# Background steps held in order on three more engines, and the q features of the down product cut into small steps

## The chip, the cores and the metric

The kernel runs on one core of one Trainium2 chip. The metric is the time of the program on the device in microseconds (us), smaller is better. The kernel before took 2384.36 us, the median of three runs (2380.04 to 2385.91).

## The reference

```
xn  = layernorm(x)                                  # x: 2048 rows of 1024
qkv = xn @ wqkv                                     # 1024 -> 3 * 1024, 32 heads of 32
pq, pk   = q @ w_phi, k @ w_phi                     # per head
phi_q = concat(softmax(pq), softmax(-pq))           # phi_k alike; 64 features a head
kv  = phi_k^T v;   z = sum over rows of phi_k
o   = (phi_q kv) / (phi_q z + 1e-6)
s   = o @ wo
h   = sigmoid(xn @ w_gate) * (xn @ w_up)            # 1024 -> 3584
g   = silu(h @ w_down)                              # 3584 -> 1024
out = x + s * g
```

All tensors are fp32.

## The kernel before, in words

**Arithmetic.** An fp32 product is three matmuls of numbers cut to a high and a low part (`mm3`, lines 142 to 144). So every operand is first split: ScalarE copies the high part (line 133), VectorE subtracts it from the source to get the low part (line 134). Each large product (x by wqkv, x by gate and up, h by down) is a seven-product Strassen-Winograd scheme over 2x2 blocks; the products are called B11, T2, T3, B21, T1, T4 and B22, and their results are added in PSUM (eight banks of 128x512) or in SBUF, some of them by way of DRAM.

**Stages, in order of time.** (1) A first list, FIRST, whose instructions stand in an order written out by hand on all engines. (2) The projection to q, k, v for one half of the rows (`PROJ`, column block c = 0). Its results are evacuated by `project`'s inner function, lines 608 to 636; ScalarE copies a bank to a buffer y (lines 612 and 620) and the y is stored to the DRAM tensor `qkv_d`. The buffers y come from a ring, `yps[0]`, of two half slots, both in slot 47. (3) Pass 0 of the gate and up products. (4) The projection for c = 1. (5) Pass 1 of gate and up, whose evacuations are `keep_bank` (ScalarE, line 1328, store to `m_d`), `seed` (ScalarE, line 1324, which fills a bank with a partial result), and `h_direct` (sigmoid on ScalarE, line 1361, product on VectorE, line 1363). (6) Pass 2 (`nest`), which finishes gate and up. (7) The down product: 112 steps `dsteps`, of 24 matmuls each up to the last product, B22, where a step has 12; `down_prep` loads and splits operands for the steps to come (tiles `x` and `w` read from slot `fa`), `evacuate` empties the banks after each product. (8) Attention, the output projection, and the output.

**Background work.** Beside the matmuls of stages 2 to 6 runs work on other data. It is cut into steps and put into a plan: `later(n, f)` runs f at the n-th `tick` from now, and `tick()` is called once for every 12 matmuls. `k_steps` (line 719) plans the chain for 128 rows of k and v: `k_load` (SyncE's DMA queue, lines 678 to 680), `k_extremes` (VectorE max and min, lines 643, 644), `k_spread` (653, 654), the exponential (ScalarE, 657), `k_inverses` (662, 663), `k_scale` (699), `k_low` (707, 709) and `kv_products` (8 matmuls, line 715). The sums of weight blocks for the Strassen scheme (GpSimd) and their loads are planned in the same way (`glu_group`, `fetch_operand`, `wd_sums`, `x_nest_load` and so on).

**Order of instructions.** Each engine, and SyncE's DMA queue, takes its instructions strictly in order. Where no list is written by hand, a scheduler sets that order from the program's order and from when it thinks an instruction can start. `tc.issue_after(x)` holds the instructions of the block, on the engine of x, behind x. Before, `tick` holds the background steps behind the last matmul, which speaks of TensorE only; during pass 0 the loads are held behind the last traced load too (`loads_after`). On VectorE, ScalarE and the queue the scheduler is free to put a background instruction ahead of instructions of the main work that were traced earlier.

**The q features in the down product.** `q_task(t, hb)` (line 930) does 128 rows by 512 columns of phi_q over its denominator: load, for half of the tasks the whole chain of features (`features`, lines 638 to 664), a product with z on GpSimd (941), a reduction and small operations on VectorE (944 to 950), a scaling on GpSimd (953) and a store. There are 32 tasks, and the step loop of the down product traces one whole task every 2.4 steps, held behind the last operand split. Both GpSimd operations cover 128x1024.

**Evacuation in the down product** (lines 1678 to 1699). B11: ScalarE copies the bank to u1. B21: a sigmoid by ScalarE from the bank and a product by VectorE with the bank (`gate_out` with `fused`, lines 1674 and 1675), for all eight banks after the last step. T2 and T3: VectorE adds bank and u1. T4: VectorE adds bank and u1 to a buffer, later a sigmoid and a product by GpSimd. The banks start afresh in B11, T2, T3 and T1 and go on adding in the others.

Of the kernel before, what the change touches and what calls it, by code (L numbers as in the profile page):

```python
# [18 lines left out]
P = 128  # L19
# [30 lines left out]
def hedgehog_glu_kernel(  # L50
# [62 lines left out]
    EARLY = 12  # L113

# [50 lines left out]
    loads_fixed = []  # L165

    def loads_after():

        return tc.issue_after(last_load[0]) if loads_fixed else nullcontext()
# [119 lines left out]
    fblock = {K: ((6, 7), (36, 37), (52, 53), (36, 37)), Q: ((50, 51), (52, 53)) * 2}  # L289
# [168 lines left out]
    def glu_group():  # L458
# [25 lines left out]
        if not groups:  # L484
            kept = [b for b in raw_free if not any(b is o for o in spare)]
            raw_free.clear()
            raw_free.extend(kept)

# [414 lines left out]
    eqr = Ring((50, 51))  # L903
    qraw = Ring([slots[53][:, 1]])
    zb = whole(54)
# [24 lines left out]
    def q_task(t, hb):  # L930
        e, ez = whole(eqr.next()), whole(52)
        if t < CTT:
            nc.sync.dma_start(e, e_d[t, hb])
            r = small.tile([P, 32], F32, name=f"r{t}{hb}", tag="r", bufs=2)
            nc.sync.dma_start(r, r_d[t, hb])
        else:
            p = qraw.next()
            nc.sync.dma_start(p, qkv_d[Q, t, hb])
            r = features(f"q{t}{hb}", p, e)
        st = small.tile([P, 5, 16], F32, name=f"sa{t}{hb}", tag="sa", bufs=2)  # L940
        nc.gpsimd.tensor_mul(ez, e, zb)  # L941
        d2 = st[:, 0:2].rearrange("p t h -> p (t h)")
        r2 = st[:, 2:4].rearrange("p t h -> p (t h)")
        nc.vector.tensor_reduce(d2, ez.rearrange("p (g d) -> p g d", d=DH), axis=AX.X, op=ALU.add)  # L944
        nc.vector.tensor_mul(d2, d2, r)  # L945
        den = st[:, 4]
        nc.vector.tensor_reduce(den, d2.rearrange("p (h t) -> p h t", t=2), axis=AX.X, op=ALU.add)
        nc.vector.tensor_scalar_add(den, den, EPS_DEN)
        nc.vector.reciprocal(den, den)
        nc.vector.tensor_mul(r2.rearrange("p (h t) -> p h t", t=2), r.rearrange("p (h t) -> p h t", t=2),  # L950
                             den[:, :, None].to_broadcast([P, 16, 2]))
        e3 = e.rearrange("p (g d) -> p g d", d=DH)
        nc.gpsimd.tensor_mul(e3, e3, r2[:, :, None].to_broadcast([P, 32, DH]))  # L953
        nc.sync.dma_start(e_d[t, hb], e)
# [438 lines left out]
    def begin_pass(p):  # L1393
# [12 lines left out]
        elif p == 1:  # L1406
            gates_r.items = halves(45, 46)
            gates_r.n = 0
            at = 1
# [15 lines left out]
    def x_nest_load(th):  # L1425
        for h in range(2):
            nc.sync.dma_start(slots[((52, 53), (43, 44))[th][h]], xr_d[T1, :, 4 * th + 2 * h:4 * th + 2 * h + 2])

    def x_nest_parts(h):

        lo, hi = slice(0, 256), slice(256, HB)
        first, second = slots[52 + h], slots[43 + h]
# [7 lines left out]
    def x_nest_split(i):  # L1440
# [8 lines left out]
        if i == T1:  # L1449
            uvfree.extend(halves(52))  # L1450
            raw_free.extend(spare)
            spare.clear()
# [81 lines left out]
    for n, (kind, c, what, i) in enumerate(ops):  # L1534
# [3 lines left out]
        if kind == "proj":  # L1538
            if n == 8 or (c and (what, i) == (PROJ[0], B11)):
                loads_fixed.clear()  # L1540
# [48 lines left out]
        if m == 0:  # L1589
# [5 lines left out]
            loads_fixed[:] = [True] if phase == 0 else []  # L1595
# [43 lines left out]
        elif phase == 1 and f == NJ - 1:  # L1639
# [5 lines left out]
            else:  # L1645
                for b in (3, 5):
                    block(f"x{b}", 4 * b, 4, F32)
                uvfree.extend(halves(12, 13, 14, 15, 20, 21, 22, 23, 51, 45, 46, 47))
                hs_r.items = halves(48, 49, 50)
# [14 lines left out]
    block("fb", 44, 3, F32R)  # L1664
# [13 lines left out]
    def evacuate(i, p):  # L1678
# [5 lines left out]
        elif i == B21:  # L1684
            gate_out(yr.next(), t, 0, b)
        elif i == T2:
            nc.vector.tensor_add(u1[p], u1[p], b)
        elif i == T3:
            nc.vector.tensor_add(u2[p], u1[p], b)
        elif i == T4:  # L1690
            y = yr.next()
            nc.vector.tensor_add(y, u1[p], b)  # L1692
            gate_out(y, t + 4, 0)
        elif i == T1:
            nc.vector.tensor_add(u2[p], u2[p], b)
            gate_out(u2[p], t + 4, 1)
# [4 lines left out]
    wd_late, wd_kept = {}, []  # L1701
    for k, j in enumerate(range(10, NJ)):
        for part in range(3):
            wd_late.setdefault(6 * k + 1 + 2 * part, []).append((j, part))

    def wd_steps(n):
        for j, part in wd_late[n]:
            if part == 0:
                wd_kept[:] = wd_parts(j, halves(43, 38))
            else:  # L1710
# [227 lines left out]
```

## Time and profile before

| what | value |
|---|---|
| median of 3 runs (lowest to highest) | 2384.36 us (2380.04 to 2385.91) |
| the profiled execution | 2383.35 us |
| its span, first to last instruction | 2381.6 us |
| TensorE (PE) busy | 2353.0 us, 99% |
| VectorE (DVE) busy | 1654.7 us, 69% |
| ScalarE (ACT) busy | 1155.2 us, 49% |
| GpSimd (POOL) busy | 1025.5 us, 43% |
| mean granted TensorE clock | 0.996 |

How to read the profile's lines: a group's row has line, engine, operation, output <- inputs, count, then busy us and mean ns of one, then idle us of the engine just before them and what ended it. In a timeline row the start and the duration in us come first; brackets at the end hold the idle time before the instruction and the instruction that released it. A row of stretches of time ("windows") has the stretch and its length, then the busy us and the instruction count of PE, PEld (weight loads), DVE, ACT and POOL, the granted TensorE clock as a share of full speed, the busy share of the DMA engines and GB/s. A matmul of 128x512 is issued about every 0.23 us; its shown duration of 0.39 us overlaps the next.

### The profile page before, as it was taken

The numbers are of one execution on the slowest core, as the hardware profiler recorded it, in microseconds if no ns is written. First come the engines' busy times: TensorE is split into PE (matmuls) and PEld (weight loads), VectorE is DVE, ScalarE is ACT, GpSimd is POOL, SyncE is SP. The second block draws the span as 40 slices with busy tenths as digits, with TensorE's granted clock in tenths as the row PEclk, the third lists the DMA queues.
The fourth block names the chain that finished last, engine by engine and source line by source line (L and its number), as shares of the span: only waits on it lengthen the run. The fifth ranks groups of instructions, "written<-read, shape, count | busy, mean of one in ns | idle before, by whom it ended". The sixth has DMA issues, their size and how long they took to land. (4 is left out here: it accounts for less than half of the span.)

```text
span 2381.6 us, 32170 instructions
## 1 busy us (share of the span) xinstructions
PE 2353.0 (99%) x10900; PEld 1958.7 (82%) x10900; DVE 1654.7 (69%) x2099; ACT 1155.2 (49%) x1814; POOL 1025.5 (43%) x673
## 2 busy tenths in 40 slices
PE   9999999999999999999999999999999999999999
PEld 8887888888888888777888878888878888888887
DVE  8615676665588844677765575666898988877776
ACT  7344554454544645545555445453433334455553
POOL 0224236711132044555431588876533334424566
PEclk9999999999999999999999999999999999999999
DMA  8788999975687787777764889889766666876665
GB/s 294 250 311 335 358 349 351 394 262 191 191 289 247 270 289 245 257 276 253 241 232 155 303 285 307 299 301 354 254 232 229 227 221 217 284 255 243 203 206 180
DMA packets 288309, 633.55 MB, mean 266 GB/s; under 512 B 36752, under 2 KB 37008, under 8 KB 283536
## 3 DMA queue, kind: packets, MB, share of 16 engines
q1 hardware_dynamic: 288144, 631.50, 76.4%
q8 instruction: 85, 1.39, 0.2%
q14 instruction: 80, 0.66, 0.1%
HBM read 378.40 MB, written 252.97 MB: 265 GB/s over the span
## 5 line engine op out<-in xcount | busy, mean ns | idle before, releaser
L142 PE MATMUL bank<-x,w 128*128 128x512 f32 x2304 | 900.8, 391 | 13.6 <-ACT fc L1328 4.5
L143 PE MATMUL bank<-x,w 128*128 128x512 f32 x2304 | 899.6, 390 | 0.2 <-DVE x L134 0.2
L144 PE MATMUL bank<-x,w 128*128 128x512 f32 x2304 | 898.2, 390 | 0.0
L134 DVE TENSOR_TENSOR w<-fa,w 128x512 fp32r<-128x512 f32 (+1 forms) x440 | 427.5, 978 | 261.0 <-ACT w L133 248.3
L142 PEld LDWEIGHTS bank<-x,w 128*128 128x128 f32 x2304 | 434.1, 188 | 107.0 <-ACT fc L1328 6.0
L144 PEld LDWEIGHTS bank<-x,w 128*128 128x128 f32 x2304 | 433.9, 188 | 90.5 <-DVE w L134 0.4
L143 PEld LDWEIGHTS bank<-x,w 128*128 128x128 f32 x2304 | 434.2, 188 | 89.1 <-DVE x L134 0.6
L133 ACT CAST w<-fa 128x512 fp32r<-128x512 f32 (+1 forms) x440 | 297.7, 680 | 364.2 <-PE bank L143 275.8
L142 PE MATMUL bank<-w,x 128*128 128x512 f32 x708 | 278.7, 394 | 7.1 <-ACT fc L620 4.7
L143 PE MATMUL bank<-w,x 128*128 128x512 f32 x708 | 276.9, 391 | 0.9 <-DVE w L1195 0.9
L144 PE MATMUL bank<-w,x 128*128 128x512 f32 x708 | 276.4, 391 | 0.0
L142 PEld LDWEIGHTS bank<-w,x 128*128 128x128 f32 x708 | 133.4, 188 | 35.5 <-ACT fc L620 5.9
L144 PEld LDWEIGHTS bank<-w,x 128*128 128x128 f32 x708 | 133.4, 188 | 28.4 <-DVE x L1185 0.3
L143 PEld LDWEIGHTS bank<-w,x 128*128 128x128 f32 x708 | 133.5, 189 | 27.3 <-DVE w L1195 1.3
L1328 ACT COPY fc<-bank 128x512 f32<-128x512 f32 x168 | 97.1, 583 | 119.2 <-PE bank L144 50.5
L941 POOL TENSOR_TENSOR fc<-fc 128x1024 f32<-128x1024 f32 x32 | 80.7, 2521 | 160.5 <-ACT fc L657 103.2
L134 DVE TENSOR_TENSOR x<-fa,x 128x512 fp32r<-128x512 f32 x112 | 115.4, 1031 | 23.9 <-ACT x L133 23.8
L133 ACT CAST x<-fa 128x512 fp32r<-128x512 f32 x112 | 69.3, 619 | 89.4 <-DMA fa<-w_down 44.7
L953 POOL TENSOR_TENSOR fc<-fc,sa 128x1024 f32<-128x1024 f32 x32 | 70.4, 2200 | 81.3 <-DVE sa L950 76.7
L134 DVE TENSOR_TENSOR p<-fc,p 128x512 fp32r<-128x512 f32 (+1 forms) x67 | 56.7, 854 | 48.9 <-ACT p L133 48.6
L657 ACT ACTIVATE fc<-fc 128x1024 f32<-128x1024 f32 x48 | 50.9, 1060 | 60.7 <-DVE fc L654 47.7
L134 DVE TENSOR_TENSOR x<-fb,x 128x1024 fp32r<-128x1024 f32 (+1 forms) x40 | 51.7, 1309 | 33.1 <-ACT x L133 32.7
(368 smaller groups left out, 3401.0 us busy)
## 6 DMA issues: line engine op xcount, KB each, us to landing
m_d<-fc SPq DMA_DIRECT2D x168, 256.0 KB, 4.4
fa<-h_d SPq DMA_DIRECT2D x84, 512.0 KB, 4.3
fa<-wf_d SPq DMA_DIRECT2D x32, 1024.0 KB, 6.4
x<-m_d SPq DMA_DIRECT2D x122, 256.0 KB, 4.7
h_d<-fc SPq DMA_DIRECT2D x98, 256.0 KB, 4.7
fc<-e_d SPq DMA_DIRECT2D x48, 512.0 KB, 4.8
fc<-qkv_d SPq DMA_DIRECT2D x80, 256.0 KB, 4.8
fa<-w_down SPq DMA_DIRECT2D x67, 256.0 KB, 4.0
```

Source lines behind the costliest of these rows:

```text
L133: nc.scalar.copy(o[0], src)
L134: i = nc.vector.tensor_sub(o[1], src, o[0].bitcast(F32))
L142: nc.tensor.matmul(o, a[0], b[0], start=first, stop=False, **kw)
L143: nc.tensor.matmul(o, a[0], b[1], start=False, stop=False, **kw)
L144: last_mm[:] = [nc.tensor.matmul(o, a[1], b[0], start=False, stop=last, **kw).ins]
L657: nc.scalar.activation(e, e, AF.Exp)
L941: nc.gpsimd.tensor_mul(ez, e, zb)
L953: nc.gpsimd.tensor_mul(e3, e3, r2[:, :, None].to_broadcast([P, 32, DH]))
L1328: nc.scalar.copy(o, banks[b])
```

## The change

Five things are edited.

1. `tick` holds the background's steps behind the latest traced instruction of VectorE, ScalarE and SyncE's queue as well as behind the last matmul (`behind`). GpSimd stays free. `loads_after` goes. `kv_products` is planned one tick later in the wide form of `k_steps`.
2. `yps[0]` gets four half slots, 47 and 51, once FIRST is done.
3. The loads, sums and splits of the x blocks for pass 2 (`x_nest_load`, `x_nest_sums`, `x_nest_split`) are planned in the last ticks of pass 1, in slots 47, 50, 51 and 53, and no more in the first ticks of pass 2.
4. `q_task` becomes `q_late`, planned in small steps, one task every 24/5 ticks, with more buffers; both GpSimd operations are cut in two halves of 128x512; the product with z has a buffer for each half of the columns. `tick` is called after each half step and each step of the down product.
5. The evacuation: each bank is emptied right after its last matmuls. In B21 VectorE copies the bank to a buffer y, ScalarE then fills the bank with u1, and the sigmoid and the product (by GpSimd) come in later ticks. T2, T3 and T4 go on adding in the bank; T2 and T3 are copied to u1 and u2 by ScalarE, T4 goes out by sigmoid from the bank and VectorE product.

```
+    BEHIND = 'DVE', 'Activation', 'SP'
...
+    @contextmanager
+    def behind():
+        latest = {}
+        for i in reversed(nc.cur_bb.bb.instructions):
+            latest.setdefault(i.engine, i)
+            if all(getattr(mybir.EngineType, e) in latest for e in BEHIND):
+                break
+        with ExitStack() as es:
+            es.enter_context(tc.issue_after(last_mm[0]))
+            for e in BEHIND:
+                es.enter_context(tc.issue_after(latest[getattr(mybir.EngineType, e)]))
+            yield
     def tick():
         clock[0] += 1
-        with tc.issue_after(last_mm[0]):
+        with behind():
             glu_group()
             nest_load()
-        for f, a in sorted(plan.pop(clock[0], []), key=lambda fa: fa[0] is fetch_operand):
-            with tc.issue_after(last_mm[0]), loads_after():
+            for f, a in sorted(plan.pop(clock[0], []), key=lambda fa: fa[0] is fetch_operand):
                 f(*a)
...
-                     (9 + wide, k_inverses), (10 + wide, k_scale), (11 + wide, k_low), (13 + wide, kv_products)):
+                     (9 + wide, k_inverses), (10 + wide, k_scale), (11 + wide, k_low), (13 + 2 * wide, kv_products)):
...
-    eqr = Ring((50, 51))
+    eqr = Ring((50, 51, 24, 25))
...
-    zb = whole(54)
+    zb = whole(54), whole(26)
...
-    def q_task(t, hb):
...
+    def q_late(at, t, hb):
...
+        def weigh():
+            for a in range(2):
+                cols = slice(a * HB, (a + 1) * HB)
+                nc.gpsimd.tensor_mul(whole(52)[:, cols], hold["e"][:, cols], zb[hb][:, cols])
...
+        def scale():
+            e3, r2 = hold["e"].rearrange("p (g d) -> p g d", d=DH), hold["sa"][:, 2:4].rearrange("p t h -> p (t h)")
+            for a in range(2):
+                gs = slice(16 * a, 16 * a + 16)
+                nc.gpsimd.tensor_mul(e3[:, gs], e3[:, gs], r2[:, gs, None].to_broadcast([P, 16, DH]))
...
+        heavy = ((5, first), (6, second), (9, lambda: exponentials(hold["e"])), (11, sums))
+        steps = ((0, load),) + heavy if t >= CTT else ((6, load),)
+        for n, f in steps + ((11, weigh), (14, density), (15, scale), (18, keep)):
+            later(at + n, f)
...
+    yps[0].items = halves(47, 51)
...
+            for n, f, *a in ((165, x_nest_load, 0), (166, x_nest_load, 1), (166, x_nest_load, 2), (171, x_nest_load, 3), (170, x_nest_sums, 0),
+                             (175, x_nest_sums, 1), (176, x_nest_split, T2), (177, x_nest_split, T3), (179, x_nest_split, T4)):
+                later(n, f, *a)
...
-            for n, f, *a in ((3, x_nest_load, 0), (3, x_nest_load, 1), (7, x_nest_sums, 0), (7, x_nest_sums, 1),
-                             (8, x_nest_split, T2), (9, x_nest_split, T3), (10, x_nest_split, T4)):
-                later(n, f, *a)
...
         elif i == B21:
-            gate_out(yr.next(), t, 0, b)
-        elif i == T2:
-            nc.vector.tensor_add(u1[p], u1[p], b)
-        elif i == T3:
-            nc.vector.tensor_add(u2[p], u1[p], b)
+            y = yr.next()
+            nc.vector.tensor_copy(y, b)
+            nc.scalar.copy(b, u1[p])
+            later(1 + (p + 1) // 2, gate_out, y, t, 0)
+        elif i in (T2, T3):
+            nc.scalar.copy((u1 if i == T2 else u2)[p], b)
         elif i == T4:
-            y = yr.next()
-            nc.vector.tensor_add(y, u1[p], b)
-            gate_out(y, t + 4, 0)
+            gate_out(yr.next(), t + 4, 0, b)
         elif i == T1:
             nc.vector.tensor_add(u2[p], u2[p], b)
-            gate_out(u2[p], t + 4, 1)
+            later(1 + 2 * p, gate_out, u2[p], t + 4, 1)
...
+    for n in range(TT):
+        for hb in range(2):
+            q_late(2 + (2 * n + hb) * 24 // 5, n // 2 + n % 2 * CTT, hb)
...
-                    j == 0 and i in (B11, T2, T3, T1), j == NJ - 1, skip_group_check=True)
+                    j == 0 and i in (B11, T1), j == NJ - 1, skip_group_check=True)
+                if j == NJ - 1:
+                    evacuate(i, p)
+            if c != cs[-1]:
+                tick()
```

The first place is VectorE's row in pass 1, at the chain for k named `stk51` (rows 128 x 5 of the second half of the columns). Lines 643 and 644 are its `k_extremes`, which read what `k_load` brings; line 1363 is the product of `h_direct`, which the banks wait for; 134 are operand splits. Before:

```order
L663 RECIPROCAL stk31_7467<-stk31_7467 128x32
L699 TENSOR_TENSOR fc_0_100<-fc_0_100,stk31_7467 128x1024
L707 TENSOR_TENSOR fc_0_100<-fc_0_100 128x1024
L643 TENSOR_REDUCE stk51_7776<-fc_0_100 128x16
L644 TENSOR_REDUCE stk51_7776<-fc_0_100 128x16
L134 TENSOR_TENSOR w_0_94<-fa_0_97,w_0_94 128x512
L1363 TENSOR_TENSOR fb_0_99<-fb_0_99,bank2_103 128x512
L1363 TENSOR_TENSOR fb_0_99<-fb_0_99,bank3_104 128x512
```

The same place now (655 and 656 are the two extremes, 1405 the product of `h_direct`, 135 a split):

```order
L1405 TENSOR_TENSOR fb_0_99<-fb_0_99,bank2_103 128x512
L674 TENSOR_REDUCE stk41_7629<-fc_0_100 128x32
L675 RECIPROCAL stk41_7629<-stk41_7629 128x32
L135 TENSOR_TENSOR p2_1_4318<-fc_0_100,p2_1_4318 128x8x64
L1405 TENSOR_TENSOR fb_0_99<-fb_0_99,bank3_104 128x512
L711 TENSOR_TENSOR fc_0_100<-fc_0_100,stk41_7629 128x1024
L655 TENSOR_REDUCE stk51_7776<-fc_0_100 128x16
L656 TENSOR_REDUCE stk51_7776<-fc_0_100 128x16
```

The extremes of `stk51` stood ahead of both products of `h_direct`; they now stand behind them, and the chain of the rows before, `stk41`, lies where they were.

The second place is ScalarE's row in the down product, between B21 and T2. Line 1674 is the sigmoid of `gate_out` from a bank, 133 are operand copies, 657 is an exponential of the q features. Before:

```order
L133 CAST w_0_94<-fa_0_97 128x512
L657 ACTIVATE fc_0_100<-fc_0_100 128x1024
L133 CAST w_0_94<-fa_0_97 128x512
L133 CAST x4_2_5757<-fa_0_97 128x512
L1674 ACT_TABLE_LOAD
L1674 ACTIVATE fc_0_100<-bank0_101 128x512
L1674 ACTIVATE fc_0_100<-bank1_102 128x512
L1674 ACTIVATE fc_0_100<-bank2_103 128x512
```

Now (1731 fills a bank with u1, 1715 is the later sigmoid of `gate_out`, which reads y):

```order
L134 CAST w_0_94<-fa_0_97 128x512
L1731 COPY bank0_101<-x0_5_11814 128x512
L1731 COPY bank1_102<-x0_5_11814 128x512
L1731 COPY bank2_103<-x0_5_11814 128x512
L134 CAST w_0_94<-fa_0_97 128x512
L134 CAST x4_2_5757<-fa_0_97 128x512
L1731 COPY bank3_104<-x0_5_11814 128x512
L1715 ACT_TABLE_LOAD
L1715 ACTIVATE fc_0_100<-fc_0_100 128x512
```

What releases a bank has moved from a sigmoid behind a table load to a plain copy; the operand copy that stood ahead of the first of them is now behind the third.

The third place is ScalarE's row between T4 and T1, as it is now (1718 is the sigmoid from a bank, 669 an exponential of the q features):

```order
L1718 ACT_TABLE_LOAD
L1718 ACTIVATE fc_0_100<-bank0_101 128x512
L1718 ACTIVATE fc_0_100<-bank1_102 128x512
L1718 ACTIVATE fc_0_100<-bank2_103 128x512
L134 CAST w_0_94<-fa_0_97 128x512
L1718 ACTIVATE fc_0_100<-bank3_104 128x512
L1718 ACTIVATE fc_0_100<-bank4_105 128x512
L1718 ACTIVATE fc_0_100<-bank5_106 128x512
L1718 ACTIVATE x6_6_11816<-bank6_107 128x512
L134 CAST w_0_94<-fa_0_97 128x512
L669 ACT_TABLE_LOAD
L669 ACTIVATE x6_6_11816<-x6_6_11816 128x1024
```

Before, no ScalarE instruction stood between the last matmuls of T4 and a free bank: VectorE's row read

```order
L134 TENSOR_TENSOR w_0_94<-fa_0_97,w_0_94 128x512 x2
L1692 TENSOR_TENSOR fc_0_100<-x0_5_11814,bank0_101 128x512
L134 TENSOR_TENSOR x4_2_5757<-fa_0_97,x4_2_5757 128x512
L1692 TENSOR_TENSOR fc_0_100<-x0_5_11814,bank1_102 128x512
L1692 TENSOR_TENSOR fc_0_100<-x0_5_11814,bank2_103 128x512
L1692 TENSOR_TENSOR fc_0_100<-x0_5_11814,bank3_104 128x512
```

and the release of a bank has gone from one VectorE addition to a sigmoid and the VectorE product behind it (line 1719).

Counted over the program: matmuls and DMAs are as many as before. ScalarE has 24 copies (1549 for 1525) and 10 table loads (76 for 66) more, GpSimd 64 products more (726 TensorTensor for 662), VectorE 24 TensorTensor fewer (1607 for 1631) and 8 copies more.

More of the change, by code (lines that the diff above doesn't have):

```diff
@@ L1663, in hedgehog_glu_kernel @@
         block(f"x{b}", 4 * b, 4, F32)
-    block("fb", 44, 3, F32R)
+    block("x6", 24, 4, F32)
+    block("fb", 44, 3, F32)
+    qraw.items = [slots[53][:, 1], slots[44][:, 0]]
+    yr.items = halves(47, 48, 49, 27)
+    eqr.items, zb = [50, 51, 24, 25], (whole(54), whole(26))
     u1, u2 = halves(0, 1, 2, 3), halves(4, 5, 6, 7)
@@ L1699, in evacuate @@
             gate_out(u1[p], t, 1)
[L1701 to L1710, printed above, removed]
-                with tc.issue_after(last_split[0]):
-                    wd_kept[part - 1]()
-    ND = len(dsteps)
-    late = [(t, hb) for hb in range(2) for n in range(CTT) for t in (n, n + CTT)]
+    ND = len(dsteps)
+    for n, j in enumerate(range(10, NJ)):
+        later(1 + 14 * n, wd_sums, j, halves(43, 38))
+    for hb in range(2):
+        later(1 + hb, nc.sync.dma_start, zb[hb], zb_d[hb])
+    for n in range(TT):
+        for hb in range(2):
+            q_late(2 + (2 * n + hb) * 24 // 5, n // 2 + n % 2 * CTT, hb)
     for n, (i, j, cs) in enumerate(dsteps):
         w, hs = dready[n]
+        if (i, j) == (T2, 0):
+            sig_r.items = [slots[53][:, 0]] + halves(38)
         for c in cs:
@@ L1738, in hedgehog_glu_kernel @@
             pass
-        if j == NJ - 1:
-            for c in cs:
-                for u in range(4):
-                    evacuate(i, 4 * c + u)
-        if n and n * 32 // 78 > (n - 1) * 32 // 78 and late:
-            t, hb = late.pop(0)
-            if t == 0:
-                nc.sync.dma_start(zb, zb_d[hb])
-            with tc.issue_after(last_split[0]):
-                q_task(t, hb)
+        tick()
         if 40 <= n < 56 and n % 2 == 0:
@@ L1751, in hedgehog_glu_kernel @@
         if n == ND - 2 * NJ:
-            assert not late and len(WO[B21]) == 4
+            assert len(WO[B21]) == 4
             block("x1", 4, 4, F32R)
```

87 lines of the change are left out of this document (46 added, 41 removed).

## The prediction

> **What bounds the kernel now.** I read the head of the page first, then what TensorE waits for, then stretches of time around those waits, then the timelines of the engines named there. TensorE bounds the kernel:
>
> ```profile
> span 2381.6 us, 32170 instructions
> PE 2353.0 (99%) x10900; PEld 1958.7 (82%) x10900; DVE 1654.7 (69%) x2099; ACT 1155.2 (49%) x1814; POOL 1025.5 (43%) x673
> ```
>
> The matmuls stay as they are, so what can be won is the 28.6 us in which PE is idle, and what matmuls lose at a lower clock. TensorE's waits (us in all, times, longest):
>
> ```profile
> PE bank L142 <- ACT fc L620: 4.7, 3, 2.9
> PE bank L142 <- ACT fc L1328: 4.5, 3, 2.6
> PE bank L142 <- ACT bank L1324: 4.4, 3, 2.2
> PE bank L142 <- DVE fc L1675: 2.9, 1, 2.9
> PE bank L142 <- ACT w L1194: 1.9, 1, 1.9
> PE bank L142 <- ACT bank L1498: 1.7, 1, 1.7
> ```
>
> The stretches in which they lie, and one without idle time that gives the pace:
>
> ```profile
> 100.00:160.00 60.00, 57.10 (x289) 48.24 (x288) 14.40 (x14) 24.99 (x37) 11.13 (x9) 0.97 0.87 306
> 160.00:300.00 140.00, 134.84 (x622) 111.19 (x622) 71.49 (x82) 64.19 (x100) 47.14 (x30) 1.00 0.92 336
> 950.00:1110.00 160.00, 151.10 (x669) 123.64 (x668) 109.43 (x110) 80.72 (x127) 90.59 (x58) 0.98 0.75 258
> 1360.00:1390.00 30.00, 27.95 (x121) 22.18 (x120) 24.87 (x27) 15.06 (x29) 24.80 (x21) 1.00 0.73 243
> 1770.00:1800.00 30.00, 27.08 (x108) 21.85 (x107) 26.36 (x40) 13.71 (x23) 8.93 (x4) 0.89 0.74 249
> 1800.00:2010.00 210.00, 210.00 (x928) 173.91 (x927) 190.06 (x279) 80.01 (x129) 77.56 (x33) 1.00 0.64 220
> ```
>
> Stretch less PE busy gives the idle time: 2.9 us (end of FIRST), 5.2 (first projection), 8.9 (pass 1), 2.05 (pass 2), 2.9 (down product), 22.0 in all. The last row has 928 matmuls in 210 us: 0.226 us a matmul. Behind some waits the granted clock is lower:
>
> ```profile
> 110.00:120.00 10.00, 8.47 (x30) 6.64 (x31) 3.27 (x4) 1.50 (x3) 3.50 (x3) 0.83 0.73 259
> 1040.00:1050.00 10.00, 7.41 (x27) 5.65 (x26) 7.05 (x6) 6.15 (x9) 5.21 (x4) 0.83 0.82 271
> 1095.00:1105.00 10.00, 7.88 (x28) 6.33 (x29) 9.69 (x8) 5.17 (x9) 8.42 (x5) 0.83 0.60 198
> 1775.00:1787.00 12.00, 9.08 (x29) 6.92 (x28) 10.54 (x16) 7.47 (x13) 2.38 (x1) 0.72 0.68 232
> ```
>
> One less the clock, by the length, is what it costs: 1.7, 1.7, 1.7 and 3.4 us, 8.5 together. 22.0 + 8.5 = 30.5 us is the most that the change can win.
>
> **The change part by part.** *The ring of y (first projection).* ScalarE's timeline:
>
> ```profile
> 194.15 0.58 ACT L620 COPY fc<-bank 128x512 f32<-128x512 f32 x1 [12.53 <-DMA qkv_d<-fc]
> 273.25 0.62 ACT L133 CAST p<-fc 128x512 fp32r<-128x512 f32 x1 [2.46 <-POOL fc L299]
> 273.77 0.58 ACT L620 COPY fc<-bank 128x512 f32<-128x512 f32 x1
> ```
>
> The copy at 194 waited for the store of the same buffer. With four buffers in place of two, that store has two more results of time. The one at 273 stood behind a background cast that waited for GpSimd; the new order holds that cast behind. All three waits go: -4.7 (0 if other waits take their place). The store's queue is unchanged, and the next matmuls need operands long split, so I see nothing late next.
>
> *End of FIRST.* The queue's and ScalarE's timelines:
>
> ```profile
> 102.03 0.32 SPq L540 DMA_DIRECT2D fa<-wf_d  x1
> 108.54 1.99 ACT L1194 CAST w<-fa 128x1024 fp32r<-128x1024 f32 x2 [5.18 <-DMA fa<-wf_d]
> ```
>
> L1194 waits for a weight load that took 6.5 us. Two background loads stood ahead of it on SyncE's queue and now stand behind FIRST's own. I take -1, between 0 and -(2.9 + 1.7) = -4.6, nearer 0 since the DMA engines are 0.87 busy there whatever the order.
>
> *Order in pass 1.* Around 1050 us, on VectorE, ScalarE and the queue:
>
> ```profile
> 1046.37 0.44 SPq L680 DMA_DIRECT2D fc<-qkv_d  x1
> 1052.32 0.69 DVE L643 TENSOR_REDUCE stk<-fc 128x16 f32<-128x512 f32 x1 [4.02 <-DMA fc<-qkv_d]
> 1054.12 1.28 DVE L1363 TENSOR_TENSOR fb<-fb,bank 128x512 f32<-128x512 f32 x2
> 1054.83 0.59 ACT L1324 COPY bank<-x 128x512 f32<-128x512 f32 x1 [6.96 <-DVE fb L1363]
> ```
>
> `k_load` is issued at 1046.4; VectorE's next row is the extremes of these very data, so it stands 4.0 us; behind it stand the products of `h_direct`, which free banks 2 and 3; behind those the seeds, ScalarE's whole queue (6.96 us), and TensorE. In the changed order these extremes come behind the products. `k_extremes` is planned four ticks after `k_load`; held to that, the load has 48 matmuls, 10.8 us, and it took 5.95 here. If it is late still, products already traced are ahead of the wait. The six waits of L1328 and L1324 are this one pattern (8.9 us) and its slow clock is 3.4 us, 12.3 in all. I take -9, between 0 and -12.3, as the late queue itself stays and main loads are in it too.
>
> *Pass 2.* ScalarE:
>
> ```profile
> 1367.66 0.62 ACT L133 CAST p<-fc 128x512 fp32r<-128x512 f32 x1 [2.25 <-POOL fc L1438]
> 1369.75 0.57 ACT L1498 COPY bank<-bank 128x512 f32<-128x512 f32 x1
> ```
>
> The cast of a summed x block waits 2.25 us for GpSimd (L1438 is `x_nest_sums`), and the seed that TensorE needs stands behind it. Loads and sums now come ahead of pass 2, their loads beside pass 1's last ones on the queue, where a late one would now hold what stands behind it in pass 1. I take -1.2 (0 to -2.05).
>
> *B21 to T2.* Timelines of the down product:
>
> ```profile
> 1756.53 2.41 DVE L134 TENSOR_TENSOR x<-fa,x 128x512 fp32r<-128x512 f32 x1
> 1775.12 0.62 ACT L133 CAST x<-fa 128x512 fp32r<-128x512 f32 x1 [2.37 <-DMA fa<-wd_d]
> 1775.76 1.28 ACT L1674 ACT_TABLE_LOAD   x1
> ```
>
> VectorE was late, as GpSimd's long q operations stretch its splits to 2.41 us; so a slot came free late, its load landed late, ScalarE's cast stood 2.37 us for it, and the table load and sigmoids that free the banks stood behind. Now banks are freed by a VectorE copy and a ScalarE copy of which three stand ahead of the next cast. I take -5.5 of 2.9 + 3.4 = 6.3 (0 to -6.3).
>
> *Work added and taken.*
>
> ```profile
> L134 DVE TENSOR_TENSOR w<-fa,w 128x512 fp32r<-128x512 f32 x365 | 330.9, 913 | 165.8 <-ACT w L133 153.2 <-PE bank L143 6.0 <-DMA xo_d<-x 4.6
> L1324 ACT COPY bank<-x 128x512 f32<-128x512 f32 x52 | 30.7, 590 | 39.5 <-DVE fb L1363 38.7
> L657 ACT ACTIVATE fc<-fc 128x1024 f32<-128x1024 f32 x48 | 50.9, 1060 | 60.7 <-DVE fc L654 47.7 <-issue 9.8 <-POOL p L866 2.9
> L657 ACT ACT_TABLE_LOAD x31 | 39.8, 1283 | 43.6 <-DVE fc L654 34.9 <-issue 8.4
> L1363 DVE TENSOR_TENSOR fb<-fb,bank 128x512 f32<-128x512 f32 x48 | 32.6, 680 | 27.5 <-PE bank L144 27.5
> L941 POOL TENSOR_TENSOR fc<-fc 128x1024 f32<-128x1024 f32 x32 | 80.7, 2521 | 160.5 <-ACT fc L657 103.2 <-DVE sa L944 35.1 <-DMA fc<-e_d 17.5
> ```
>
> ScalarE gets 24 copies of 0.59 and 10 table loads of 1.28, 27 us; it is busy 80 of 210 us in the down product, so they cost nothing while it has such room, and at most 27 without. VectorE loses 24 operations and gains 8 copies of about 0.68, 11 us less where it is 90% busy. GpSimd does the same elements in halves (2.52 us becomes two of about 1.26), busy 78 of 210; that shortens the longest stretch of a split and is worth nothing by itself.
>
> *T4 to T1, new.* From bank 0's last matmul in T4, the third of its step, to T1's first on bank 7 are 42 matmuls, 9.5 us. In ScalarE's new row stand there: three table loads (3.85), eight sigmoids taken as copies (4.7), two casts (1.2), one exponential (1.06), then VectorE's product (0.68): 11.5 us. That is 2.0 late, or 0.7 if the first table load runs ahead of the matmul. I take +1.5 (0 to +5, were the exponential to wait for a VectorE at 90%).
>
> [...]
>
> *Other new waits.* A background held strictly behind three engines starts later on each, and what reads it can be late: sums of weights, k chains, x splits. Nothing in the trace shows this order; its nearest rows are the waits above, 1.7 to 2.9 us each. I take one, +2.5 (0 to +12, four with slow clock).
>
> *Sum*: -4.7 - 1 - 9 - 1.2 - 5.5 + 1.5 + 2.5 = -17.4. From the profiled 2383.35 that is 2365.95; the median of the runs lies 1.0 higher: **2367.0**. With the last term between its ends, 2364 to 2377.
>
> **The rivals.** Differences under 0.3%, 7.2 us, cannot be told from none: faster is below 2377.2, slower above 2391.5.
>
> *Every wait goes and none comes*: -30.5 gives 2354 (2353.85 with the 1.0). For it speaks that each wait has a cause which the change touches; against it, that DMA is 0.87 to 0.92 busy at the first two.
>
> *The clock stays low in places*: idle time goes, slow clock stays. The first projection's wait of 2.9 us left its stretch at 1.00, and 2.9 at 1778 made 0.72, so the drop isn't in the wait's length alone. Of the 3.4 in pass 1 the sum holds about 2.5 (9 of 12.3), of the 3.4 in the down product about 3.0 (5.5 of 6.3); without these 5.5 the time is 2372.5. [...]
>
> *The waits only move*: loads stay late, and a main split waits where a background reduction did. Then -4.7 from the ring and nothing else, with +2.5 and +1.5: 2383.
>
> *Slower: k chains late at their matmuls.* `kv_products` are matmuls in TensorE's row; late features stop everything.
>
> ```profile
> L707 DVE TENSOR_TENSOR fc<-fc 128x1024 f32<-128x1024 f32 x30 | 43.0, 1433 | 0.6
> L709 DVE TENSOR_TENSOR p<-fc,p 128x1024 fp32r<-128x1024 f32 x32 | 47.3, 1477 | 4.0 <-ACT p L700 3.9
> ```
>
> Between `k_low`, tick 12, and the products, now tick 15, lie 36 matmuls, 8.1 us. VectorE has there L707 and L709 (2.9), two of L1363 (1.4) and three splits (2.7): 7.0 us, room of 1.1. If GpSimd stretches two splits to the 2.41 above, 10.0 us: 1.9 late, 20 chains in pass 1, +38 and 2405. It decides from 1.2 us late each, 24 us. Against it: pass 1's row shows VectorE busy 109 of 160, and the extra tick gives 2.7 us of the room.
>
> **How the numbers follow.** The forecast 0.55; every wait gone 0.10; low clock 0.10; waits only move 0.12; slower 0.13. Faster: 0.55 + 0.10 + 0.10 = 0.75, same 0.12, slower 0.13. The range runs from 2354, all gained, to 2385, the moved waits with some room: all but the slower rival and the tails.
>
> **What would show it.** Right: no waits of L620, none on the seeds and `keep_bank` copies in pass 1, extremes that wait while PE is busy, clock 1.00 at 1050, 1100 and 1778, no wait between B21 and T2, and one of 1 to 2 us between T4 and T1. Wrong: waits for line 711 to 721's results at `kv_products`, a wait of TensorE for splits of x or w in pass 1 or the down product, or PE idle above 20 us in all.

## The result, and the profile after

The changed kernel took 2373.14 us (median of 5 runs, 2369.56 to 2375.03) against 2382.85 us for the kernel before (5 runs, 2380.04 to 2385.91): a ratio of 0.9958, 95% interval 0.9944 to 0.9973. Forecast was 2367.0, in 2354 to 2385. The profiled span went from 2381.6 to 2371.4 us, 10.2 less.

The head of the page of the changed kernel, and what TensorE waits for (us in all, times, longest):

```profile
span 2371.4 us, 32110 instructions
PE 2348.0 (99%) x10900; PEld 1958.6 (83%) x10900; DVE 1649.0 (70%) x2083; ACT 1182.1 (50%) x1848; POOL 1046.7 (44%) x737
```

```profile
PE bank L143 <- ACT bank L1538: 7.0, 2, 4.9
PE bank L143 <- ACT bank L1553: 6.2, 1, 6.2
PE bank L375 <- DMA fb<-wqkT: 1.7, 1, 1.7
...
PE bank L1026 <- DMA fc<-e_d: 1.3, 2, 1.1
```

None of the six rows shown of before is left. In their place stand two lines, 1538 and 1553: ScalarE's seeds of banks in pass 2. The stretches, read as before (stretch, length, busy us and counts of the five engines, granted clock, DMA share):

```profile
160.00:300.00 140.00, 140.00 (x642) 116.56 (x641) 70.52 (x75) 67.83 (x105) 53.68 (x36) 1.00 0.93 341
...
950.00:1110.00 160.00, 160.00 (x730) 133.33 (x729) 111.09 (x113) 86.68 (x133) 97.22 (x63) 1.00 0.84 292
...
1520.00:1580.00 60.00, 53.02 (x216) 42.85 (x215) 29.08 (x40) 25.18 (x47) 44.06 (x37) 0.91 0.87 301
1580.00:1640.00 60.00, 53.79 (x232) 44.10 (x231) 26.15 (x35) 20.50 (x37) 39.98 (x29) 0.94 0.81 303
...
1770.00:1800.00 30.00, 30.00 (x134) 24.84 (x133) 30.00 (x43) 23.32 (x37) 19.86 (x14) 1.00 0.61 212
```

The first projection, pass 1 and the step from B21 to T2 are full now, at clock 1.00. The end of pass 2 has 13.2 us of idle time and clocks of 0.91 and 0.94, which is 5.4 and 3.6 us if one less the clock is taken by the length. Some 2.8 of these 9.0 us lie in the idle time itself (clock 0.82 from 1554 to 1559 us, 0.73 from 1595 to 1602 us), in which no matmul runs; that leaves 13.2 + 6.2 = 19.4 us, an estimate from these rows. This stretch had no idle time before.

The start of one and the same matmul in both traces gives a ledger: where the difference (after less before) changes for good, time was won or lost. It does so at these places:

| place | forecast | measured |
|---|---|---|
| start of the program | 0 | +0.8 |
| end of FIRST (110 us) | -1 | -4.9 |
| load of `wqkT` (145 us) | 0 | +1.9 |
| first projection | -4.7 | -6.6 |
| pass 1 | -9 | -14.0 |
| start of pass 2 | -1.2 | -2.6 |
| end of pass 2 | in +2.5 | +19.5 |
| T2 to T3 (1693 us) | in +2.5 | +0.5 |
| B21 to T2 | -5.5 | -6.0 |
| T4 to T1 and the rest of the down product | +1.5 | -0.7 |
| attention | 0 | +1.9 |
| sum | -17.4 | -10.2 |

So every gain came, and more than its share: 34.8 us with the -0.7 of the down product. One new cost, at the end of pass 2, took back 19.5.

**What makes the new wait.** ScalarE's timeline of the changed kernel, ahead of the longest wait of L1538:

```profile
1553.82 0.62 ACT L134 CAST w<-fa 128x512 fp32r<-128x512 f32 x1 [6.52 <-POOL fa L526]
...
1558.46 0.56 ACT L1538 COPY bank<-bank 128x512 f32<-128x512 f32 x1
```

The cast takes a sum of gate and up weights (`nest_load`, lines 518 to 527) that GpSimd delivers late, and the seed stands behind it. So GpSimd's waits in pass 2 (1340 to 1610 us) are what to read: the rows of the changed kernel that wait for transfers, and then all such of the kernel before:

```profile
POOL fa L524 <- DMA fa<-wg_d: 23.4, 3, 8.4
POOL fc L875 <- DMA fc<-w_down: 21.6, 4, 9.4
...
POOL fa L524 <- DMA fb<-wg_d: 3.7, 1, 3.7
...
POOL fb L524 <- DMA fa<-wg_d: 2.3, 1, 2.3
...
POOL fc L1385 <- DMA x<-m_d: 1.4, 1, 1.4
```

```profile
POOL fc L1343 <- DMA h_d<-fc: 4.1, 1, 4.1
...
POOL fc L863 <- DMA fc<-w_down: 2.1, 1, 2.1
```

52.4 us in place of 6.2. GpSimd and SyncE's queue show why, around 1450 us:

```profile
1446.39 0.45 SPq L1392 DMA_DIRECT2D h_d<-fc  x1
1446.93 0.91 SPq L518 DMA_DIRECT2D fa<-wg_d  x2
...
1449.17 0.57 SPq L520 DMA_DIRECT2D fb<-wg_d  x1
1457.14 0.32 SPq L1382 DMA_DIRECT2D h_d<-fb  x1
```

```profile
1445.05 1.30 POOL L1388 TENSOR_TENSOR fc<-x,fc 128x512 f32<-128x512 f32 x1
1453.29 0.88 POOL L524 TENSOR_TENSOR fa<-fa 128x256 f32<-128x256 f32 x1 [6.93 <-DMA fa<-wg_d]
...
1455.83 1.28 POOL L1415 TENSOR_TENSOR fb<-fb,x 128x512 f32<-128x512 f32 x1
```

The queue issues the weight load (L518) right behind a store (L1392) that waited for GpSimd's L1388. GpSimd, which is not held, has the sum of these weights (L524) next, ahead of the product L1415, so it stands 6.9 us for the load. The next store (L1382) needs L1415, so the queue stands from 1449.7 to 1457.1 (6.5 us of it are a wait for L1415), and with it every load behind that store. Queue and GpSimd wait for each other in turn, in lock step, and GpSimd falls behind until a cast that TensorE's seed stands behind has to wait.

### The profile page after: what moved, and what is told of

Read it like the earlier page. It is cut to its first block, busy times and chain, and to the rows that moved or that the text cites. A ratio compares the mean times of both kernels' runs of the same rounds, so it can differ in the third digit from the quotient of the medians.

```text
span 2371.4 us, 32110 instructions
## 1 busy us (share of the span) xinstructions
PE 2348.0 (99%) x10900; PEld 1958.6 (83%) x10900; DVE 1649.0 (70%) x2083; ACT 1182.1 (50%) x1848; POOL 1046.7 (44%) x737
## 4 chain that ended last, share of the span: by engine, by line
PE 93%; DMA 2%; POOL 1%; DVE 1%; issue 1%; ACT 1%; SPq 0%; POOLq 0%; DVEq 0%; ACTq 0%
PE bank L143 29%; PE bank L144 29%; PE bank L145 29%; PE bank L727 1%; PE bank L375 1%; PE bank L1050 1%; PE bank L1026 1%; PE bank L1300 1%; DMA fc<-w_down 1%; DMA fc<-e_d 1%; DMA h_d<-x 0%; DMA fb<-wqkT 0%; PE bank L243 0%; POOL x L1415 0%; DMA fc<-qkv_d 0%
## 5 line engine op out<-in xcount | busy, mean ns | idle before, releaser
L135 DVE TENSOR_TENSOR w<-fa,w 128x512 fp32r<-128x512 f32 (+2 forms) x437 | 426.8, 984 | 371.5 <-ACT w L134 363.0
L134 ACT CAST w<-fa 128x512 fp32r<-128x512 f32 (+2 forms) x437 | 296.6, 682 | 445.2 <-PE bank L144 345.6
L135 DVE TENSOR_TENSOR x<-fa,x 128x512 fp32r<-128x512 f32 x112 | 105.0, 938 | 28.1 <-ACT x L134 27.8
L135 DVE TENSOR_TENSOR w<-fb,w 128x512 fp32r<-128x512 f32 (+1 forms) x45 | 40.3, 894 | 48.6 <-ACT w L134 48.6
L1064 POOL TENSOR_TENSOR fc<-fc 128x512 f32<-128x512 f32 x32 | 48.9, 1528 | 56.3 <-DVE fc L1059 20.7
L135 DVE TENSOR_TENSOR p<-fc,p 128x512 fp32r<-128x512 f32 (+1 forms) x67 | 52.2, 790 | 30.6 <-ACT p L134 29.7
L135 DVE TENSOR_TENSOR x<-fb,x 128x1024 fp32r<-128x1024 f32 x36 | 46.1, 1282 | 28.8 <-ACT x L134 28.7
L306 POOL TENSOR_TENSOR fb<-fb 128x512 f32<-128x512 f32 x6 | 8.4, 1396 | 126.3 <-DMA fb<-w_gu 116.9
```

What stands on the lines that cost most here:

```text
L134: nc.scalar.copy(o[0], src)
L135: i = nc.vector.tensor_sub(o[1], src, o[0].bitcast(F32))
L1064: nc.gpsimd.tensor_sub(o, a, b)
```

## The experiments

Theory 1 is this lock step. Rivals: theory 2, the x blocks of pass 2 in other slots leave fewer buffers; theory 3, the strict order on VectorE and ScalarE. Times come with their ratio to the kernel before on the same chip.

**Queue free in pass 2** (`sp_free_pass2`).

```
-            for e in BEHIND:
+            for e in BEHIND if phase != 2 else BEHIND[:2]:
```

> The changed kernel, but in pass 2 background steps are held behind the latest VectorE and ScalarE instructions only, not behind SyncE's queue. Theory 1 (lock step): in pass 2 the queue's weight loads stand behind stores that wait for GpSimd, and GpSimd's sums wait for these loads, with the products that the stores need behind them. Then GpSimd's idle time for DMA in 1340 to 1600 us (about 58 us in all) falls under 10, the three new TensorE waits of 2.0, 4.9 and 6.2 us and their slow clock go, and the time falls by about 19.5 us, from 2373 to about 2354. Theory 2 (buffers: the x blocks of pass 2 sit in other slots, so pass 2 starts with fewer free buffers) and theory 3 (order on VectorE and ScalarE): no change, 2373, the three waits stay.

2352.06 us, ratio 0.9865 (0.9850 to 0.9879). The three waits are gone (TensorE waits for nothing in pass 2), and GpSimd's waits for transfers fall from 52.4 to 5.3 us. The time is 22 us less than that of the changed kernel by the two ratios, which is theory 1's number; theories 2 and 3 fall as the cause, since slots and the order on VectorE and ScalarE are unchanged here.

**Queue free everywhere** (`sp_free_all`).

```
-    BEHIND = 'DVE', 'Activation', 'SP'
+    BEHIND = 'DVE', 'Activation'
```

> The changed kernel, with SyncE's queue taken out of the engines that background steps are held behind, everywhere. Theory 1: as with the queue free in pass 2 alone, the three waits of pass 2 go (-19.5 us); if the queue's order is what also won the waits at the end of FIRST (4.9 us) and in pass 1 (14 us), these come back: 2354 if neither does, 2359 if FIRST's does, 2373 if both do. Theories 2 and 3: the three waits stay, 2373 or more.

2371.68 us, 0.9949 (0.9933 to 0.9966): the waits of pass 2 go, and others come back. TensorE's waits, and ScalarE ahead of the first of them:

```profile
PE bank L143 <- ACT fc L1370: 5.3, 1, 5.3
...
PE bank L143 <- ACT w L1235: 2.2, 1, 2.2
...
PE bank L143 <- DVE fb L618: 2.1, 1, 2.1
```

```profile
1065.06 0.58 ACT L1370 COPY fc<-bank 128x512 f32<-128x512 f32 x1 [14.13 <-DMA m_d<-fc]
```

In pass 1 a copy of `keep_bank` waits 14.1 us for the store of its own buffer, since background transfers stand ahead of that store; one of them, a store of line 882, held the queue for 2.1 us until GpSimd had its data. Two more waits are new there: 2.2 us at `kv_products` (line 727), for VectorE, and 2.6 us at line 764, for GpSimd. So while GpSimd is free, the queue's order is worth about as much outside pass 2 as it costs inside.

**GpSimd held too** (`pool_held`).

```
-    BEHIND = 'DVE', 'Activation', 'SP'
+    BEHIND = 'DVE', 'Activation', 'SP', 'Pool'
```

> The changed kernel, with GpSimd added to the engines that background steps are held behind. Theory 1: GpSimd's sums that wait for loads now stand behind the products of the main work traced before them, so stores leave, loads go out and the lock step breaks: the three waits fall from 13.2 us to under 5, time 2354 to 2362. If the late load alone counts (the queue's order) and not what GpSimd does meanwhile, the waits stay: 2373. Theories 2 and 3: 2373.

2350.51 us, 0.9859 (0.9844 to 0.9874), a little under the range. GpSimd's wait for transfers in pass 2, and TensorE's waits of the whole program:

```profile
POOL fc L875 <- DMA fc<-w_down: 0.2, 1, 0.2
```

```profile
PE bank L1300 <- POOL ident masks.py:199: 1.5, 1, 1.5
PE bank L143 <- DVE x L1741: 0.8, 1, 0.8
PE bank L1026 <- DMA fc<-e_d: 0.7, 1, 0.7
```

52.4 us became 0.2, with the queue held as in the changed kernel. Breaking the lock step on either side is enough. This version beats both kernels.

**X blocks as before** (`x_nest_old`). Their loads, sums and splits go back to pass 2's first ticks, with the slots of before.

```
-            for n, f, *a in ((165, x_nest_load, 0), (166, x_nest_load, 1), (166, x_nest_load, 2), (171, x_nest_load, 3), ...
+            for n, f, *a in ((3, x_nest_load, 0), (3, x_nest_load, 1), (7, x_nest_sums, 0), (7, x_nest_sums, 1), ...
-        first, second = slots[(47, 51)[h]], slots[(50, 53)[h]]
+        first, second = slots[52 + h], slots[43 + h]
```

> The changed kernel, with the loads, sums and splits of the x blocks for pass 2 put back to the first ticks of pass 2, in the slots of before. Theory 1: the three late waits of pass 2 stay, and the wait of some 2.6 us at the start of pass 2 comes back: about 2376. Theory 2: the three waits go and that one comes back: 2373 - 19.5 + 2.6 = 2356. Theory 3: as theory 1.

2367.75 us, 0.9931 (0.9916 to 0.9946). Neither number: the wait at the start came back (3.6 us), and those at the end of pass 2 halved (3.6, 0.9 and 2.1 us). GpSimd's waits for transfers fell from 52.4 to 30.6 us. So the early x blocks made the lock step worse here; whether by slots or by traffic is open. They are not its cause: the order alone, below, has the lock step without them.

**VectorE and ScalarE free** (`queue_pool_only`).

```
-    BEHIND = 'DVE', 'Activation', 'SP'
+    BEHIND = 'SP', 'Pool'
```

> The changed kernel, with background steps held behind the latest instructions of SyncE's queue and GpSimd only; VectorE and ScalarE are free as before. The forecast's theory: what won pass 1 is that k_extremes no longer stand ahead of h_direct on VectorE; then pass 1's waits come back, 9 us idle and 14 us in all, and the time is about 2364 (2350.5 with all four held, plus 14). Rival: what won pass 1 is the order of SyncE's queue (loads and stores of the main work no longer stand behind background ones); then it stays at 2350 to 2354.

2385.53 us, 0.9988 (0.9978 to 0.9998), some 31 us above the kernel with all four held, and neither number. By the ledger against that kernel, 8.9 us come back in pass 1, in place of 14 (waits of 1.3, 1.2 and 3.5 us). There the extremes wait for their loads again; from 940 to 1115 us, in the kernel before and here:

```profile
DVE stk L643 <- DMA fc<-qkv_d: 22.2, 5, 5.6
```

```profile
DVE stk L655 <- DMA fc<-qkv_d: 28.2, 7, 7.2
```

In the changed kernel, and with the queue free everywhere, VectorE has no such wait there. The second projection has a wait of 3.6 us (at 782 us), and the down product three large ones, among them:

```profile
PE bank L143 <- ACT x L1734: 8.1, 2, 6.0
...
PE bank L143 <- ACT bank L1731: 4.8, 1, 4.8
```

VectorE and ScalarE ahead of the wait of 6.0 at 1932 us:

```profile
1926.07 0.69 DVE L655 TENSOR_REDUCE stq<-fb 128x16 f32<-128x512 f32 x1 [2.70 <-DMA fb<-qkv_d]
```

```profile
1929.60 1.06 ACT L669 ACTIVATE x<-x 128x1024 f32<-128x1024 f32 x1 [7.43 <-DVE x L666]
...
1931.59 1.55 ACT L1734 COPY x<-bank 128x512 f32<-128x512 f32 x3
```

This is the forecast's mechanism, in another stage too: extremes that wait for their load, an exponential behind them, and the copy that frees the bank behind that.

**The order alone** (`order_alone`), on the kernel before.

```
-        with tc.issue_after(last_mm[0]):
+        with behind():
...
-                     (9 + wide, k_inverses), (10 + wide, k_scale), (11 + wide, k_low), (13 + wide, kv_products)):
+                     (9 + wide, k_inverses), (10 + wide, k_scale), (11 + wide, k_low), (13 + 2 * wide, kv_products)):
```

> The kernel before with the order alone: background steps held behind the latest VectorE, ScalarE and queue instructions as well, and kv_products a tick later; ring, x blocks and down product as before. Lock step theory: FIRST -4.9 and +2 behind it, pass 1 -14, one wait of the first projection -1.9, and the new waits of pass 2 +19.5: together about 0, 2386. Rival (the new waits need the x blocks' early loads too): without them about 2367. In the down product its q tasks stand held behind the last split as before, so its wait of 2.9 us stays.

2385.88 us, 1.0002 (0.9992 to 1.0012), the expected time, though in part by luck. Its trace has no wait in the first projection or pass 1, and 4.2, 4.3, 3.3 and 1.0 us in pass 2, where GpSimd's waits for transfers come to 44.6 us: the lock step is there without the early x blocks. By the ledger against the kernel before, the first projection gains 6.3 us where 1.9 were expected. The down product loses 9.2 us that were not expected: its wait at B21 is 6.9 us, no longer 2.9, and two waits for splits are new (2.6 and 1.2 us, at 1671 and 1678 us).

**The ring alone** (`ring_alone`), on the kernel before.

```
-    fblock = {K: ((6, 7), (36, 37), (52, 53), (36, 37)), Q: ((50, 51), (52, 53)) * 2}
+    fblock = {K: ((6, 7), (36, 37), (52, 53), (36, 37)), Q: ((50, 38), (52, 53)) * 2}
...
+    yps[0].items = halves(47, 51)
```

> The kernel before with four buffers y in the first projection in place of two (and the block of w_phi's product that used slot 51 in slot 38). Theory of the forecast: the two waits of the first projection for a store go (2.9 and about 0.5 us, with what the matmuls behind them lose about 4.8 us), the one at 274 us behind a background cast stays: 2385.6 - 4.8 = about 2381. Rival: all three go, -6.6, 2379. If the waits only move: 2385.

2385.31 us, 0.9995 (0.9985 to 1.0004). The wait of the first projection stays, with another reason. ScalarE with the ring of four:

```profile
196.37 0.62 ACT L133 CAST p<-fc 128x512 fp32r<-128x512 f32 x1 [10.70 <-DMA fc<-wo]
196.90 0.58 ACT L620 COPY fc<-bank 128x512 f32<-128x512 f32 x1
```

The copy needs no store now, but stands behind a background cast. ScalarE and the queue of the kernel before show why the store had been late:

```profile
180.02 0.61 ACT L620 COPY fc<-bank 128x512 f32<-128x512 f32 x1
```

```profile
176.41 10.31 SPq L370 DMA_DIRECT2D wf_d<-fc  x7
...
187.40 0.41 SPq L599 DMA_DIRECT2D qkv_d<-fc  x1
```

Seven background stores, and a load, went ahead of it: it left 6.8 us after its copy had ended at 180.6. With the order alone the same copy and the same store stand at

```profile
175.64 0.59 ACT L628 COPY fc<-bank 128x512 f32<-128x512 f32 x1 [0.62 <-PE bank L145]
```

```profile
177.90 1.08 SPq L607 DMA_DIRECT2D qkv_d<-fc  x1
```

which is 1.7 us after the copy's end. ScalarE still waits 7.1 us for that store, but TensorE does not wait: a ring of two is then enough.

**The down product alone** (`down_alone`): the changed kernel with the other parts undone, so that ticks are held behind the last matmul only.

```
-        with behind():
+        with tc.issue_after(last_mm[0]):
...
-    yps[0].items = halves(47, 51)
```

> The kernel before with the new down product alone: small q steps, new evacuation, a tick after each step, but ticks held behind the last matmul only. Forecast: the wait of 2.9 us at B21 to T2 and its slow clock go, -6 us, 2380, with at most 1.5 us at T4 to T1. Rival: in free order the q steps stand ahead of operand splits and a wait of the same size comes elsewhere in the down product: 2386.

2440.06 us, 1.0230 (1.0213 to 1.0247): 53 us slower than before, far worse than the rival. TensorE waits 16.7 us once, 11.8 us once, and ten times for splits. VectorE and ScalarE ahead of the longest:

```profile
1810.08 0.68 DVE L649 TENSOR_REDUCE stq<-fb 128x16 f32<-128x512 f32 x1
1810.67 1.45 DVE L135 TENSOR_TENSOR w<-fa,w 128x512 fp32r<-128x512 f32 x1
1812.04 0.68 DVE L1724 COPY fc<-bank 128x512 f32<-128x512 f32 x1
```

```profile
1812.75 0.59 ACT L1725 COPY bank<-x 128x512 f32<-128x512 f32 x1 [10.12 <-DVE fc L1724]
```

Free, the small q steps fill VectorE's row ahead of the copy that empties bank 0. The new down product and the order belong together: without the order the first is harmful, without the first the order leaves the wait at B21. Whether the harm comes from the small q steps or from the new evacuation was not run apart.

**The remaining four** hold GpSimd too, with one part each put back. `kv_products` at the tick of before (`pool_kv_early`):

```
-    ... (13 + 2 * wide, kv_products)):
+    ... (13 + wide, kv_products)):
```

> All four engines' rows held (the kernel pool_held), with kv_products planned at the tick of before, one earlier. The forecast's slower rival: held chains come late at their matmuls; by its count the tick is 2.7 us of room and 20 chains hang on it, so each would be up to 1.6 us late: +10 to +32 us over pool_held's ratio of 0.986. If the chains have room without it: no change, 0.985 to 0.987.

2350.6 us, 0.9850 (0.9834 to 0.9867), no wait at the products. With GpSimd held, the later `kv_products` was not needed.

The x blocks in pass 2's first ticks (`pool_x_old`), by the diff shown above:

> All four engines' rows held, with the x blocks of pass 2 loaded, summed and split in its first ticks as before. With the lock step broken, only the wait at the start of pass 2 should come back: 2 to 4 us, ratio 0.987 to 0.988. If the early x loads are harmful by themselves (x_nest_old was 4 us faster than the changed kernel): no slower than pool_held, 0.984 to 0.986.

2357.21 us, 0.9876 (0.9861 to 0.9891); one wait of 4.0 us at 1348 us, none later in pass 2. Without the lock step the early x blocks are worth 5.6 us at the start of pass 2, by the ledger against the kernel with all four held.

The queue free (`queue_free_pool_held`):

```
+    BEHIND = 'DVE', 'Activation', 'Pool'
```

> The changed kernel with background held behind VectorE, ScalarE and GpSimd, and SyncE's queue free. If the queue's order is what wins the end of FIRST, the first projection and pass 1: the waits there of sp_free_all stay (2.2 + 0.9, 2.1 and 5.3 us, about 15 us in all), ratio 0.992 to 0.995, and no wait in pass 2. If holding GpSimd alone repairs these: 0.986.

2361.94 us, 0.9897 (0.9882 to 0.9912), between the two: waits of 1.5 + 0.9, 2.5 and 0.8 us stay at the end of FIRST, in the first projection and at `kv_products`; the one of 5.3 in pass 1 is gone. By the ledger the queue's order is then still worth 4.6 us at the end of FIRST and 4.2 in the first projection, but 1.1 in pass 1.

Two buffers y (`pool_ring_of_2`):

```
-    yps[0].items = halves(47, 51)
```

> All four engines' rows held, with two buffers y in the first projection as before (slot 47 only). The forecast's theory: the ring of four wins the waits of the first projection, 4.7 us; then they come back, ratio 0.988. Rival, from order_alone: the order of the queue wins them, as stores then leave on time; then no wait of TensorE there and a ratio of 0.985 to 0.987.

2353.5 us, 0.9859 (0.9836 to 0.9882): the ratio of four buffers, in an interval 11 us wide. The trace decides: the first projection has one wait, 0.7 us, for the input of a background product, and none for a store, and takes 1.3 us longer than with four. The order wins that stage, not the ring.

## Why the prediction was right and where it was not

**The sum** was -17.4 and came out at -10.2 in the profiles, with the sign and the range right. The parts were off in both directions. That the total still lies in the range is in part luck: the five gains came to 34.1 us where 21.4 were forecast, the new costs to 24.6 us where 4.0 were. One of the prediction's own signs of being wrong came true: TensorE is idle for 2371.4 - 2348.0 = 23.4 us, above the 20 that it named.

**The term that failed** is "other new waits, I take one, +2.5 (0 to +12)". It measured +19.5 at the end of pass 2 alone, beyond its end, and about 4 more elsewhere. The prediction saw that a held step starts later, and priced it by the waits of before; it did not ask which engine was left free. GpSimd was, and its sums depend on the queue that is now held. Holding GpSimd too (`pool_held`) and freeing the queue in pass 2 (`sp_free_pass2`) show both halves of that.

**The first projection**: -4.7 forecast, -6.6 measured, for the wrong reason. The step "with four buffers that store has two more results of time" fails in `ring_alone` (nothing gained) and `pool_ring_of_2` (nothing lost). The row read "waits for the store"; why that store was late stood on the queue, and I did not look there. Only the wait at 273 us was put down to the order.

**FIRST**: the mechanism was right (the wait is back with the queue free), the size wrong: -4.9 for -1. The weight load left 1.5 us earlier and took 4.9 us in place of 6.5. A busy DMA share of 0.87 was no reason to take the gain near 0; it is 0.87 from 100 to 160 us in the changed kernel too.

**Pass 1**: -14.0 for -9, beyond the -12.3 at its end. The pattern was right: with VectorE and ScalarE free the extremes wait for their loads again, and 8.9 us come back. In the changed kernel they don't wait at all, so the sign "extremes that wait while PE is busy" did not show. It is not the whole: with the queue and GpSimd free 12.2 us come back although the extremes don't wait, and with the queue alone free 1.1. So pass 1 needs the order on VectorE and ScalarE, and on the queue or GpSimd as well. The bound of 12.3 was too low, and not because of the clock: all matmuls that ran 0.43 us apart, six from 1044.3 and seven from 1098.5 us, lie in its two stretches. What it leaves out is about 0.3 us around each wait: the last matmul ahead of it is shown for 0.39 us, where the next would start after 0.23, and the first one behind it takes 0.34 to the next. That is some 1.7 us for six waits. So the 30.5 us called the most that can be won is too low as well; with GpSimd held the profiled span is 2348.3 us, 33.3 less than before.

**Start of pass 2**: -2.6 for -1.2, for the reason given; with the x blocks put back the wait is back (3.6 and 4.0 us). **B21 to T2** came in the forecast size, -6.0 for -5.5, but the new evacuation alone, which it was put down to, does not bring it: without the order (`down_alone`) this part of the down product is slower than before.

**T4 to T1** was put at +1.5 and showed no wait. The first table load began at 1994.1 us, for the most part ahead of the end of bank 0's last matmul (1995.1), the case for which 0.7 was named. Its second table load:

```profile
1999.96 1.28 ACT L669 ACT_TABLE_LOAD   x1
2001.25 1.06 ACT L669 ACTIVATE x<-x 128x1024 f32<-128x1024 f32 x1
```

The cast ahead of it ended at 1999.94 us, so nothing but the 1.28 us shows. The last product of T4 ended at 2004.95 us, as TensorE came to its bank, so there was no room for more: had a switch cost more, TensorE would have waited here, and it didn't. The other two loads of this place (1994.10 and 2002.34 us) and the one of the kernel before (1775.76 us) take 1.28 us as well, and each begins within 0.03 us of the end of the instruction ahead of it. So these traces show 1.28 us a switch.

**The rivals.** "The waits only move" was half right: 13.2 us of waits moved to pass 2. (Its sum, 2383, lacks the 1.0 us that the other sums add; with it 2384.) "Clock stays low" is out: the stretches of pass 1 and B21 are at 1.00, and the clock fell only behind the new waits. "K chains late" is out for the changed kernel: no wait at the products, and with all four held (`pool_kv_early`) they have room even without the added tick. With the queue free they do wait, 2.2 us, and 0.8 with GpSimd held. "Every wait goes", 2354, is about what the change gives once GpSimd is held: 2350.5.

## What to carry to other kernels

When background work is held in order, hold it on every engine in its chain: one free engine that waits for a held queue, while the queue's next store waits for that engine, took back 19.5 us here, where the order had won some 25 (FIRST, first projection and pass 1). When a row says that an instruction waited for a transfer, look at the queue for what stood ahead of that transfer before giving it more buffers. And change the size of steps and their order together: the down product's small steps without the order were harmful (1.0230). That the order alone came to 1.0002 doesn't show that it is worth nothing, since that run has the lock step in it; the order alone with GpSimd held was not run.

## What the chip showed beside this

The granted clock fell behind some short waits and not behind others. In the changed kernel TensorE stood 2.04 us at 1531.8; 1.5 us later each matmul took 0.43 us where it had taken 0.23 (clock 0.79 from 1531 to 1535 us):

```profile
1531.81 0.50 PE L143 MATMUL bank<-x,w 128*128 128x512 f32 x1 [2.04 <-ACT bank L1538]
...
1533.07 0.41 PE L145 MATMUL bank<-x,w 128*128 128x512 f32 x1
...
1534.13 0.63 PE L145 MATMUL bank<-x,w 128*128 128x512 f32 x1
1534.56 0.63 PE L143 MATMUL bank<-x,w 128*128 128x512 f32 x1
```

Waits of 1.7 us at 145 us and 0.8 us at 2159 left it alone (1.00 from 140 to 160 and from 2155 to 2163 us), and so did the 2.9 us at 194 us in the kernel before, where the matmuls behind the wait are 0.23 us apart. So in these traces the length of one wait does not decide it; what does is open.
